# Three layers on one core: the order of the second layer's operands, one pair of weights split from PSUM, and two weight tiles converted ahead

## The chip, the cores and the metric

The kernel runs on one core of a Trainium2 chip. The metric is the time of the device in microseconds (us), the median of several executions. The engines are called as in the profile: PE (TensorE, matrix products; PEld its weight loads), DVE (VectorE), ACT (ScalarE), POOL (GpSimd) and SP (SyncE, which issues the transfers). Each engine works through its own list of instructions in order and waits where an instruction needs another engine's result.

## The reference

```python
def reference(q, k, v, p, w_in, w_out, w_gate, w_val, w_out2):      # shortened
    # q, k, v: (4, 8, 576, 64); p: (4, 8, 32, 64)
    pp = sm_attn(p, k, v)                       # softmax attention, 32 packed rows
    a = sm_attn(q, pp, pp)                      # (4, 8, 576, 64)
    x = a.transpose(0, 2, 1, 3).reshape(2304, 512)
    h = x @ w_in                                # 512 x 2048
    x = softplus(h) @ w_out                     # 2048 x 512
    return (sigmoid(x @ w_gate) * (x @ w_val)) @ w_out2   # 512 x 1536, 1536 x 512
```

The inputs of the attention are float32, the five weights are float64.

## The kernel before

**Precision.** A product is made of three matmuls on fp32r operands: each operand x is split in hi, a copy rounded to fp32r, and lo = x - hi, and `mm3` adds hi·hi, hi·lo and lo·hi. `split_lo` (line 99) is the subtraction, on VectorE or GpSimd. The weights come in as float64 bits; `convert` makes float32 of a block with three integer operations on VectorE (lines 178, 183, 187), 128x512 each.

**First layer.** The batch b and the half s of its tokens select 288 tokens; `emit_h(b, c, s)` makes 256 of the 2048 columns of h (chunk c, eight chunks) and `emit_out1` adds their share of the output to `xa` (six matmuls, then the addition of line 658 on VectorE, four PSUM banks in turn). The second attention product and w_in are joined: instead of x, the kernel takes the attention weights (A2h, A2l) and multiplies them by pp @ w_in, which `prep_wp_one` (one batch) or `prep_wp_two` (two batches, a "half") makes for each chunk: four small matmuls for either of two banks (line 587), then hi and lo of the result (wph, wpl). In `prep_wp_two` ScalarE copies PSUM to SBUF (cv, line 594), GpSimd makes hi (line 102) and GpSimd makes lo (line 99). From chunk 2 on the batches go in two halves (batches 0, 1 and batches 2, 3), chunk by chunk.

**Second layer.** For each pair of f (128 columns of w_gate and of w_val; twelve f) and each half ps of the batches, x @ w_gate and x @ w_val are made together from seven products of half size and additions (Strassen's scheme as Winograd orders it). With x of a batch as four quarters x11, x12 (first half of the tokens) and x21, x22 (second half), the operands of the tokens' side ("A operands", tiles aop) are A11 = x11, A12 = x12, A22 = x22, S1 = x21 + x22, S2 = S1 - x11, S4 = x12 - S2 and S3 = x11 - x21; `prep_A(b)` makes the four sums on VectorE (line 705), all hi on ScalarE (line 698) and all lo on VectorE, that of A22 on GpSimd. The weights' side (BH, BL) comes from `blocks(f)`, which converts three raw tiles (raw_g, raw_v, raw_o), builds four further blocks with GpSimd subtractions and stores the result to a scratch in DRAM for the second half, and from `prep_B(ps, f)`, which reloads the scratch if there is one and splits it (GpSimd: hi of some, all lo; w_out2's are oh and ol). `emit_gv` multiplies in the order A11, S2, S3, S1, A12, A22, S4; each product needs one of three double banks, which VectorE's additions (lines 927, 939) and ScalarE's copies set free. `emit_out2` multiplies the gated result gv by w_out2's block, twice 128 columns at a time, and adds it to `xa` (line 982).

**What sets the order.** The work of preparation is written as generators in the queues `jobs` and `idle`; `tick()`, called after each piece of TensorE's work, takes one step of the first job, so a job that stands ahead delays those behind it. Blocks for the f in the list `EARLY` are converted ahead, in layer 1, from chunk 4 on. The tile framework's scheduler then puts the instructions of each engine in its own order, so the order in the program isn't that of the source. At the passage from ps = 0 to ps = 1, f = 11 is done batch by batch, and `prep_A` of batches 2 and 3 is put in the queue behind batch 0 and 1.

Of the kernel before, what the change touches and what calls it, by code (L numbers as in the profile page):

```python
# [9 lines left out]
F32 = mybir.dt.float32  # L10
# [3 lines left out]
ALU = mybir.AluOpType  # L14
# [6 lines left out]
def attn_moe_moe_kernel(  # L21
# [21 lines left out]
    nc = tc.nc  # L43
# [5 lines left out]
    P = 128  # L49
    NC = 6  # L50
    CT = S // NC
    HS = S // 2
# [14 lines left out]
    XR = 0  # L67
    VCH = 8
    VSP = 0
    EARLY = [0]  # L70
    NCV = 5
    SC = float(D) ** -0.5

# [55 lines left out]
    later = {f: [(nm, f // 2, f % 2) for nm in ("g", "v", "o2")] for f in range(2 * NCH2)}  # L129
    early = list(EARLY)  # L130
    order, early_in = [], {}
# [114 lines left out]
    jobs = deque()  # L246
# [42 lines left out]
    WPP = 1  # L289
    WPH = 0  # L290
    SPL = []
    SP0 = []
    ALO = ['A22']
    EV2 = EM2 = EM1 = [nc.vector, nc.vector]
    EGL = [nc.gpsimd, nc.vector]
    HIA = [5, 9]
# [242 lines left out]
    def x2(b, s):  # L539

        i = KD * HS * (2 * b + s)
        return xa[:, i : i + KD * HS].rearrange("p (m t) -> p m t", m=KD)
# [35 lines left out]
    def prep_wp_two(half, c):  # L578
        wt = w_in_f[c]
        hl = [wp_tiles() for _ in range(2)]  # L580
        if WPP:
            xs = [new_cv().rearrange("p (t n) -> p t n", t=2) for _ in range(2)]
        for par in range(2):
            ps = bank1().rearrange("p (t n) -> p t n", t=2)
            for t in range(2):
                j = 2 * t + par
                nc.tensor.matmul(  # L587
                    ps[:, t, :], bdT[:, 4 * half + j, :], wt[:, j, :], start=True, stop=True
                )
            yield  # L590
            for e in range(2):
                r = slice(64 * e, 64 * e + 64)
                if WPP:
                    nc.scalar.activation(xs[e ^ par][r], ps[r], AF.Copy)
                else:
                    hi, lo = hl[e ^ par]
                    nc.scalar.activation(hi[r], ps[r], AF.Copy)
                    split_lo(nc.vector, lo[r], ps[r], hi[r])
                yield
            yield  # L600
        if WPP:
            for (hi, lo), x in zip(hl, xs):
                hi_of(WPH, hi, x)
                split_lo(nc.gpsimd, lo, x, hi)
                yield
        for x in range(2):
            Wp[2 * half + x, c] = hl[x]
# [69 lines left out]
    w2 = []  # L677
    NF = NCH2 * 2
    HB = B // 2
    Aop, Bop, scratch, gv = {}, {}, {}, {}  # L680

    def prep_A(b):
        pool = w2[0] if b % 2 == 0 else big
        n = 11 if pool is big else 7
        Aop[b] = {}
        for nms in (("A11", "A12"), ("A22", "S1"), ("S2", "S3"), ("S4",)):
            tiles = [
                pool.tile([P, 2, 2, HS], F32R, tag="big", bufs=n, name="aop")
                for _ in range(len(nms))
            ]  # L690
            for e, nm in enumerate(nms):
                Aop[b][nm] = [tiles[0][:, e], tiles[-1][:, 1 if len(nms) == 1 else e]]
        x11, x12 = x2(b, 0)[:, :2], x2(b, 0)[:, 2:]
        x21, x22 = x2(b, 1)[:, :2], x2(b, 1)[:, 2:]

        def split(nm, x):
            hi, lo = Aop[b][nm]
            nc.scalar.activation(hi, x, AF.Copy)
            split_lo(nc.gpsimd if nm in ALO else nc.vector, lo, x, hi)

        def sum_():
            return w2[0].tile([P, 2, HS], F32, tag="sum", name="sum")

        def tt(to, x, y, op):
            nc.vector.tensor_tensor(to, x, y, op=op)

        split("A11", x11)
        yield
        split("A12", x12)
        yield  # L710
        split("A22", x22)
        yield
        t = sum_()
        tt(t, x21, x22, ALU.add)
        yield
        split("S1", t)
        yield
        tt(t, t, x11, ALU.subtract)
        yield
        split("S2", t)  # L720
        yield
        tt(t, x12, t, ALU.subtract)
        yield
        split("S4", t)
        yield
        t = sum_()
        tt(t, x11, x21, ALU.subtract)
        yield
        split("S3", t)
        yield  # L730


# [49 lines left out]
    def prep_B(ps, f):  # L782

        if f in scratch:
            parts = [new_cv(), new_cv()[:, :CF], new_cv(), new_cv(), new_cv()]
            for x, a, n in places(parts):
                nc.sync.dma_start(x, scratch[f][:, a : a + n])
        else:
            parts = yield from blocks(f)
        yield  # L790
        pool = w2[f % 2]
        hi = pool.tile([P, 7 * CF], F32R, tag="BH", name="BH")
        lo = pool.tile([P, 7 * CF], F32R, tag="BL", name="BL")
        oh = wo_p.tile([P, DM], F32R, tag="woh", bufs=4, name="oh")
        ol = wo_p.tile([P, DM], F32R, tag="wol", bufs=4, name="ol")
        for x, a, n in places(parts):
            h, l = (oh, ol) if a == 7 * CF else (y[:, a : a + n] for y in (hi, lo))
            hi_of(HIA[ps] * 100 > a, h, x)
            split_lo(nc.gpsimd, l, x, h)
            yield  # L800
        Bop[ps, f] = (
            hi.rearrange("p (j n) -> p j n", n=CF), lo.rearrange("p (j n) -> p j n", n=CF),
            oh, ol,
        )
# [27 lines left out]
    for i, (b, c) in enumerate(entries):  # L832
        if c == 0:
            while not att_done(2 * b + 1):
                att_tick()
            if b:
                for cc in range(2):
                    jobs.appendleft((f"wp{b}{1 - cc}", prep_wp_one(b, 1 - cc)))
        if (b, c) == (3, 0):
            jobs.append(("win2", prep_win(2)))  # L840
        if (b, c) == (3, 1):
            jobs.append(("wp02", prep_wp_two(0, 2)))
        if c >= 2 and b % 2 == 0:
            k = groups.index((b // 2, c))
            if k == 0:
                jobs.append(("wo2", prep_wo(2)))
            if k + 1 < len(groups):
                x, cc = groups[k + 1]
                jobs.append((f"wp{2 * x}{cc}", prep_wp_two(x, cc)))
            if k + 2 < len(groups) and weights and groups[k + 2][1] == weights[0]:  # L850
                cc = weights.popleft()
                jobs.extend(idle)
                idle.clear()
                jobs.append((f"win{cc}", prep_win(cc)))
                jobs.append((f"wo{cc}", prep_wo(cc)))
                idle.append((f"early{cc}", prep_early(early_in.get(cc, ()))))
            if (b, c) == BAT:
                jobs.extend(idle)
                idle.clear()
                jobs.append(("B00", prep_B(0, 0)))  # L860
        for x in range(2):
            if (b, c) == (x + 2, NCH1 - 2):
                jobs.append((f"A{x}", prep_A(x)))
        if (b, c) == CPC:
            cps[0] = CPS > 0
        if (b, c) == (1, 2):
            att.release()
            w2.append(tc.alloc_tile_pool(name="w2", bufs=1, side="right"))
        finish(f"wp{b}{c}" if c < 2 else f"wp{b - b % 2}{c}")
        for s in range(2):  # L870
            emit_h(b, c, s)
            pace = 0
            for bb in range(b + 1, B if c < 2 else 0):
                slots = 3 * (4 * bb - 2 * i - s) - MARGIN
                pace = max(pace, -(-att_left(2 * bb + 1) // max(1, slots)))
            ticks = [pace] * 3
            if len(pend) == DEPTH:
                emit_out1(*pend.popleft(), ticks)
            else:
                for m in range(KD):  # L880
                    between(m, ticks)
            pend.append((b, c, s))
# [119 lines left out]
    for i, (ps, f) in enumerate(steps):  # L1002
        finish(f"B{ps}{f}")
        if i + 1 < len(steps):
            n_ps, n_f = steps[i + 1]
            jobs.append((f"B{n_ps}{n_f}", prep_B(n_ps, n_f)))
        whole = list(range(HB))
        first_last = f in (SPL if ps else (SP0 + [NF - 1]))
        for n, group in enumerate([[p] for p in whole] if first_last else [whole]):
            for p in group:  # L1010
                finish(f"A{HB * ps + p}")
            emit_gv(ps, f, group)
            if ps == 0 and f == NF - 1:
                jobs.appendleft((f"A{HB + n}", prep_A(HB + n)))
            some_out2(LEFT if n or not first_last else LEFT0)
        if f % 2:
            todo.extend((ps, f // 2, t) for t in range(NTT))
            spread[0] = -DEL
# [37 lines left out]
```

## Time and profile before

| what | value |
|---|---|
| time, median of 3 runs (lowest to highest) | 868.61 us (866.66 to 870.32) |
| profiled execution: time / span | 866.77 / 864.7 us |
| TensorE (PE) busy, granted clock | 839.6 us (97%), 1.000 |
| weight loads (PEld) busy | 789.6 us (91%) |
| VectorE (DVE) busy | 614.6 us (71%) |
| ScalarE (ACT) busy | 401.1 us (46%) |
| GpSimd (POOL) busy | 473.2 us (55%) |

The span is the time from the first to the last instruction that the trace holds. Busy times of different engines overlap. An engine that is busy for a part of the span can still be the one that is waited for in some stretch; that is read from the waits of that stretch. The first layer's last addition lies at 435.9 us, the passage from ps = 0 to ps = 1 between 616 and 655 us.

### The profile page before, as it was taken

Reading aid. Unit: us, or ns where it says so; the run is one execution under the profiler, and the core shown is the slowest. Engines: PE = TensorE matmul, PEld = TensorE weight load, DVE = VectorE, ACT = ScalarE, POOL = GpSimd, SP = SyncE. Lnnn points to the kernel's source line nnn. Section 1 sums busy time; section 2 is a strip of 40 time slices with the busy share of each in tenths; the row PEclk is TensorE's granted clock in tenths of the full one; section 3 lists DMA queues with packets and bytes.
Section 4 is the critical chain, followed back from the end, with each engine's and each line's share of the span. In section 5 each row is a group of like instructions: output and inputs, shape, how many; then the busy total and the mean of one; then the engine's idle time right before and its main releaser. Section 6 shows DMA issues by size and latency. Waiting matters only on the chain.

```text
span 864.7 us, 15615 instructions
## 1 busy us (share of the span) xinstructions
PE 839.6 (97%) x6100; PEld 789.6 (91%) x6100; DVE 614.6 (71%) x1047; ACT 401.1 (46%) x721; POOL 473.2 (55%) x455
## 2 busy tenths in 40 slices
PE   6899999999999999999999999999989999999997
PEld 5788999989999999999999999999869999999995
DVE  1875556757576767758898688897898756767665
ACT  4567565566666666677633422232342532322210
POOL 4454233346565545576479787796883634536400
PEclk9999999999999999999999999999999999999999
DMA  9983330113032402300057464554434212213004
GB/s 233 229 221 84 80 83 2 50 49 99 1 98 92 135 21 79 123 30 1 1 167 215 134 192 148 170 136 157 140 95 137 79 45 86 67 43 111 14 1 109
DMA packets 58009, 85.55 MB, mean 99 GB/s; under 512 B 6352, under 2 KB 39248, under 8 KB 57936
## 3 DMA queue, kind: packets, MB, share of 16 engines
q1 hardware_dynamic: 57648, 84.49, 34.5%
q8 instruction: 48, 0.79, 0.4%
q14 instruction: 25, 0.20, 0.1%
q10 hardware_dynamic: 288, 0.07, 0.0%
HBM read 65.67 MB, written 18.87 MB: 98 GB/s over the span
## 4 chain that ended last, share of the span: by engine, by line
PE 84%; DVE 7%; DMA 3%; ACT 2%; POOL 2%; issue 1%; SPq 0%; POOLq 0%; ACTq 0%; DVEq 0%
PE bank L113 9%; PE bank L111 9%; PE bank L112 9%; PE ps L650 7%; PE ps L651 7%; PE ps L653 7%; PE ps L976 5%; PE ps L975 5%; PE ps L974 5%; PE ps L113 4%; PE ps L111 4%; PE ps L112 4%; PE ps L587 2%; DVE aop L99 2%; PE ps L464 2%; PE ps L348 1%
## 5 line engine op out<-in xcount | busy, mean ns | idle before, releaser
L111 PE MATMUL bank<-aop,BH 128*128 128x288 f32 x672 | 198.7, 296 | 2.8 <-DVE work L927 1.1
L112 PE MATMUL bank<-aop,BH 128*128 128x288 f32 x672 | 197.9, 295 | 1.0 <-DVE aop L99 0.9
L113 PE MATMUL bank<-aop,BL 128*128 128x288 f32 x672 | 198.7, 296 | 0.1
L99 POOL TENSOR_TENSOR ghl<-g,ghl 128x576 fp32r<-128x576 f32 x64 | 93.7, 1464 | 131.5 <-ACT ghl L106 131.5
L658 DVE TENSOR_TENSOR xa<-xa,ps 128x288 f32<-128x288 f32 x224 | 98.1, 449 | 75.4 <-PE ps L653 75.3
L650 PE MATMUL ps<-ghl,woh 128*128 128x288 f32 x512 | 148.6, 305 | 1.6 <-DVE xa L658 1.5
L651 PE MATMUL ps<-ghl,wol 128*128 128x288 f32 x512 | 143.2, 295 | 0.0
L111 PEld LDWEIGHTS bank<-aop,BH 128*128 128x128 f32 x672 | 126.2, 188 | 8.0 <-issue 1.2
L112 PEld LDWEIGHTS bank<-aop,BH 128*128 128x128 f32 x672 | 126.4, 188 | 5.1 <-DVE aop L99 1.6
L113 PEld LDWEIGHTS bank<-aop,BL 128*128 128x128 f32 x672 | 126.5, 188 | 0.4 <-POOL BL L99 0.4
L99 POOL TENSOR_TENSOR BL<-cv,BH 128x512 fp32r<-128x512 f32 (+1 forms) x96 | 117.7, 1242 | 7.2 <-ACT BH L106 6.1
L653 PE MATMUL ps<-ghl,woh 128*128 128x288 f32 x512 | 109.1, 294 | 0.0
L650 PEld LDWEIGHTS ps<-ghl,woh 128*128 128x128 f32 x512 | 96.2, 188 | 4.1 <-DVE xa L658 1.3
L651 PEld LDWEIGHTS ps<-ghl,wol 128*128 128x128 f32 x512 | 96.3, 188 | 0.6
L927 DVE TENSOR_TENSOR work<-work,bank 128x576 f32<-128x576 f32 (+1 forms) x100 | 70.9, 724 | 28.6 <-PE bank L113 28.1
L974 PE MATMUL ps<-oh,gv 128*128 128x512 f32 x216 | 84.6, 392 | 1.3 <-DVE xa L982 0.8
L975 PE MATMUL ps<-ol,gv 128*128 128x512 f32 x216 | 84.8, 393 | 0.0
L976 PE MATMUL ps<-oh,gv 128*128 128x512 f32 x216 | 84.7, 393 | 0.0
L653 PEld LDWEIGHTS ps<-ghl,woh 128*128 128x128 f32 x512 | 82.2, 188 | 0.0
L982 DVE TENSOR_TENSOR xa<-xa,ps 128x512 f32<-128x512 f32 x90 | 61.5, 684 | 27.1 <-PE ps L976 26.6
L956 ACT ACTIVATE work<-bank 128x576 f32<-128x576 f32 (+1 forms) x25 | 15.8, 634 | 137.4 <-DVE bank L927 137.4
L113 PE MATMUL ps<-A2h,wpl 128*128 128x288 f32 x256 | 76.2, 297 | 2.4 <-POOL wpl L99 2.0
(123 smaller groups left out, 1743.6 us busy)
## 6 DMA issues: line engine op xcount, KB each, us to landing
cv<-B SPq DMA_DIRECT2D x52, 256.0 KB, 2.6
B<-cv SPq DMA_DIRECT2D x48, 256.0 KB, 3.8
raw_in<-in_moe_w_in_dram SPq DMA_DIRECT2D x16, 512.0 KB, 3.6
raw_out<-in_moe_w_out_dram SPq DMA_DIRECT2D x16, 512.0 KB, 3.6
raw_g<-in_moe_w_gate_dram SPq DMA_DIRECT2D x12, 512.0 KB, 4.2
raw_v<-in_moe_w_val_dram SPq DMA_DIRECT2D x12, 512.0 KB, 4.4
raw_o<-in_moe_w_out_dram SPq DMA_DIRECT2D x12, 512.0 KB, 4.1
xa<-in_q_dram SPq DMA_DIRECT2D x6, 576.0 KB, 6.5
```

The costliest lines, as they stand in the source:

```text
L99: eng.tensor_tensor(lo, x, hi.bitcast(F32), op=ALU.subtract)
L111: nc.tensor.matmul(ps, wh, xh, start=first, stop=False)
L112: nc.tensor.matmul(ps, wh, xl, start=False, stop=False)
L113: nc.tensor.matmul(ps, wl, xh, start=False, stop=last)
L650: nc.tensor.matmul(out_, wh[:, ms], gh[:, f], start=f == 0, stop=False)
L651: nc.tensor.matmul(out_, wl[:, ms], gh[:, f], start=False, stop=False)
L653: nc.tensor.matmul(out_, wo_hl[c, f][0][:, ms], gl[:, f], start=False, stop=f == 1)
L658: nc.vector.tensor_tensor(dst, dst, out_, op=ALU.add)
L927: nc.vector.tensor_tensor(to, x, y, op=ALU.add)
L974: nc.tensor.matmul(bank, gh[:, ts_], oh, start=f == 0, stop=False)
L975: nc.tensor.matmul(bank, gh[:, ts_], ol, start=False, stop=False)
L976: nc.tensor.matmul(bank, gl[:, ts_], oh, start=False, stop=f == 1)
```

## The change

`EARLY` becomes `[0, 1]`, so the blocks of f = 0 and of f = 1 are converted in layer 1 (f = 1 in the chunks that follow those of f = 0), stored to the scratch and reloaded by `prep_B(0, 1)`. `prep_wp_two` takes the splits straight from PSUM for half 0, chunk 2 only: ScalarE writes hi and VectorE subtracts it from PSUM. In `prep_A` the operands are made in the order in which `emit_gv` multiplies by them. S2 is made in place of x21 by a new job `fold_A` (two operations); S3 = x22 - S2 and S1 = S2 + x11 follow from it. That is five sums and folds for each batch instead of four. The jobs F0 and F1 stand right ahead of A0 and A1; F2 and F3, for batches 2 and 3, are queued at f = 3 and f = 5 of ps = 0.

```diff
-    EARLY = [0]
+    EARLY = [0, 1]
...
+    FOLD = {3: 2, 5: 3}
...
     def prep_wp_two(half, c):
...
-        if WPP:
+
+        far = WPP and (half, c) != (0, 2)
+        if far:
             xs = [new_cv().rearrange("p (t n) -> p t n", t=2) for _ in range(2)]
...
-                if WPP:
+                if far:
                     nc.scalar.activation(xs[e ^ par][r], ps[r], AF.Copy)
                 else:
                     hi, lo = hl[e ^ par]
...
-        if WPP:
+        if far:
             for (hi, lo), x in zip(hl, xs):
...
+    def fold_A(b):
+
+        x11, x12, x21, x22 = quarters(b)
+        tt(x21, x21, x22, ALU.add)
+        yield
+        tt(x21, x21, x11, ALU.subtract)
+        yield
+
     def prep_A(b):
...
-        for nms in (("A11", "A12"), ("A22", "S1"), ("S2", "S3"), ("S4",)):
+        for nms in (("A11", "S2"), ("S3", "S1"), ("A12", "A22"), ("S4",)):
...
         split("A11", x11)
         yield
+        split("S2", s2)
+        yield
+        t = sum_(x22, s2, ALU.subtract)
+        yield
+        split("S3", t)
+        yield
+        t = sum_(s2, x11, ALU.add)
+        yield
+        split("S1", t)
+        yield
         split("A12", x12)
         yield
         split("A22", x22)
         yield
-        t = sum_()
-        tt(t, x21, x22, ALU.add)
...
+        t = sum_(x12, s2, ALU.subtract)
         yield
         split("S4", t)
-        yield
-        t = sum_()
-        tt(t, x11, x21, ALU.subtract)
-        yield
-        split("S3", t)
         yield
...
+                jobs.append((f"F{x}", fold_A(x)))
                 jobs.append((f"A{x}", prep_A(x)))
...
+        if ps == 0 and f in FOLD:
+            jobs.append((f"F{FOLD[f]}", fold_A(FOLD[f])))
```

In the whole program VectorE has 8 rows of instructions more (987 to 995), SyncE 7 more, ScalarE and GpSimd one each, TensorE as many as before. What the scheduler makes of it is shown at three places; the number ahead of a row is its place in the engine's list. The line numbers of the new program are higher by 3 to 14: its 590, 653 to 656, 661 are the old 587, 650 to 653, 658, its 690 the old 705, its 941, 953 and 996 the old 927, 939 and 982.

First, TensorE at the weights of chunk 6, half 0. A row with w_in is the second product pp @ w_in, ghl with woh is out1, A2h with wph is an H block. Before:

```order
1596 L587 MATMUL ps_4304<-w_in,bdT 128x256 x2
1597 L650 MATMUL ps_4307<-ghl,woh 128x288
1598 L651 MATMUL ps_4307<-ghl,wol 128x288
...
1602 L111 MATMUL ps_4316<-A2h_100,wph 128x288
1603 L112 MATMUL ps_4316<-A2l_104,wph 128x288
...
1646 L650 MATMUL ps_4392<-ghl,woh 128x288
...
1661 L111 MATMUL ps_4442<-A2h_97,wph 128x288
1662 L112 MATMUL ps_4442<-A2l_101,wph 128x288
1663 L113 MATMUL ps_4442<-A2h_97,wpl 128x288
```

And in the new program:

```order
1644 L590 MATMUL ps_4398<-w_in,bdT 128x256 x2
1645 L653 MATMUL ps_4418<-ghl,woh 128x288
1646 L654 MATMUL ps_4418<-ghl,wol 128x288
...
1660 L653 MATMUL ps_4449<-ghl,woh 128x288
1661 L654 MATMUL ps_4449<-ghl,wol 128x288
1662 L653 MATMUL ps_4449<-ghl,woh 128x288
...
1665 L111 MATMUL ps_4465<-A2h_97,wph 128x288
1666 L112 MATMUL ps_4465<-A2l_101,wph 128x288
1667 L113 MATMUL ps_4465<-A2h_97,wpl 128x288
```

Before, two H blocks of another batch (A2h_100) and eight out1 tiles stand between the product with w_in and the first H block with the new weights (A2h_97), 72 matmuls; now four out1 tiles do, 24 matmuls.

Second, VectorE at the end of layer 1, among the additions of the last out1 tiles (xa<-xa,ps). Before:

```order
577 L632 SCALAR_TENSOR_TENSOR g_5449<-ps_5405,t_5418 128x576
578 L705 TENSOR_TENSOR sum<-xa 128x576
579 L658 TENSOR_TENSOR xa<-xa,ps_5456 128x288
580 L658 TENSOR_TENSOR xa<-xa,ps_5466 128x288
581 L99 TENSOR_TENSOR aop<-sum,aop 128x576
582 L658 TENSOR_TENSOR xa<-xa,ps_5474 128x288
...
586 L178 TENSOR_SCALAR ps_5556<-raw_g 128x512
587 L658 TENSOR_TENSOR xa<-xa,ps_5506 128x288
588 L183 SCALAR_TENSOR_TENSOR ps_5556<-raw_g,ps_5556 128x512
589 L658 TENSOR_TENSOR xa<-xa,ps_5514 128x288
590 L658 TENSOR_TENSOR xa<-xa,ps_5522 128x288
```

In the new program:

```order
589 L635 SCALAR_TENSOR_TENSOR g_5481<-ps_5436,t_5449 128x576
590 L661 TENSOR_TENSOR xa<-xa,ps_5488 128x288
591 L661 TENSOR_TENSOR xa<-xa,ps_5498 128x288
592 L690 TENSOR_TENSOR sum<-xa 128x576
593 L99 TENSOR_TENSOR aop<-xa,aop 128x576
594 L661 TENSOR_TENSOR xa<-xa,ps_5508 128x288
595 L99 TENSOR_TENSOR aop<-sum,aop 128x576
596 L661 TENSOR_TENSOR xa<-xa,ps_5518 128x288
...
600 L661 TENSOR_TENSOR xa<-xa,ps_5550 128x288
601 L178 TENSOR_SCALAR ps_5730<-raw_g 128x512
602 L661 TENSOR_TENSOR xa<-xa,ps_5558 128x288
603 L183 SCALAR_TENSOR_TENSOR ps_5730<-raw_g,ps_5730 128x512
```

Before, one A operand's split and a sum stand behind the last `g` (the softplus, line 632 or 635), and then the conversion of f = 1's raw_g; now two splits and a sum follow a sum, and the conversion is that of f = 2 and comes with the last addition.

Third, VectorE at the passage from ps = 0 to ps = 1, from the first A operand of batch 2 on (work and bank are the additions behind products, xa<-xa,ps of 128x512 is the second layer's output). Before:

```order
806 L99 TENSOR_TENSOR aop<-xa,aop 128x576
807 L927 TENSOR_TENSOR work<-work,bank 128x288 x2
808 L99 TENSOR_TENSOR aop<-xa,aop 128x576
809 L982 TENSOR_TENSOR xa<-xa,ps_7704 128x512
810 L927 TENSOR_TENSOR bank<-work,bank 128x288
811 L99 TENSOR_TENSOR aop<-sum,aop 128x576
812 L982 TENSOR_TENSOR xa<-xa,ps_7722 128x512
813 L927 TENSOR_TENSOR bank<-work,bank 128x288
814 L705 TENSOR_TENSOR sum<-sum,xa 128x576
815 L982 TENSOR_TENSOR xa<-xa,ps_7740 128x512
816 L939 TENSOR_TENSOR work<-work,bank 128x288
```

In the new program:

```order
811 L99 TENSOR_TENSOR aop<-xa,aop 128x576 x2
812 L996 TENSOR_TENSOR xa<-xa,ps_7689 128x512
813 L941 TENSOR_TENSOR work<-work,bank 128x288 x3
814 L99 TENSOR_TENSOR aop<-sum,aop 128x576
815 L996 TENSOR_TENSOR xa<-xa,ps_7720 128x512
816 L941 TENSOR_TENSOR bank<-work,bank 128x288
817 L690 TENSOR_TENSOR sum<-xa 128x576
818 L996 TENSOR_TENSOR xa<-xa,ps_7738 128x512
819 L99 TENSOR_TENSOR aop<-sum,aop 128x576
820 L941 TENSOR_TENSOR bank<-work,bank 128x288
821 L99 TENSOR_TENSOR aop<-xa,aop 128x576
```

The operands of batch 2 stood in the order A11, A12, S1, with S2's sum behind; now A11 and S2 come at once, then S3, S1 and A12.

## Rows read from the trace of the kernel before

**Rows 1.** TensorE's waits: engine, line, releaser: us in total, times, longest.

```profile
PE ps L113 <- POOL wpl L99: 2.0, 1, 2.0
...
PE ps L650 <- DVE xa L658: 1.5, 3, 0.6
...
PE bank L111 <- DVE xa L658: 0.7, 1, 0.7
...
PE bank L111 <- POOL ol L99: 0.5, 1, 0.5
```

**Rows 2.** Stretches: TensorE, weight load, VectorE, ScalarE, GpSimd busy; clock; DMA share; GB/s.

```profile
620.00:660.00 40.00, 36.60 (x208) 31.36 (x207) 37.12 (x53) 13.79 (x27) 24.55 (x19) 1.00 0.40 116
660.00:680.00 20.00, 20.00 (x153) 20.00 (x152) 16.75 (x20) 8.44 (x16) 14.25 (x12) 1.00 0.32 92
```

**Rows 3.** Timeline of TensorE, chunks 2 and 6 of half 0: start, us, instruction [idle before].

```profile
173.27 1.02 PE L587 MATMUL ps<-w_in,bdT 128*128 128x256 f32 x4
173.94 0.49 PE L650 MATMUL ps<-ghl,woh 128*128 128x288 f32 x1
...
177.52 0.29 PE L653 MATMUL ps<-ghl,woh 128*128 128x288 f32 x1
179.81 0.40 PE L113 MATMUL ps<-A2h,wpl 128*128 128x288 f32 x1 [2.00 <-POOL wpl L99]
...
333.96 1.02 PE L587 MATMUL ps<-w_in,bdT 128*128 128x256 f32 x4
```

**Rows 4.** Timeline of ScalarE, chunk 2 of half 0.

```profile
174.67 1.19 ACT L594 ACTIVATE cv<-ps 64x512 f32<-64x512 f32 x2
```

**Rows 5.** Timeline of GpSimd, chunks 2 and 6 of half 0.

```profile
175.94 1.21 POOL L102 TENSOR_SCALAR wph<-cv 128x512 fp32r<-128x512 f32 x2 [2.97 <-PE ps L653]
177.12 1.42 POOL L99 TENSOR_TENSOR ghl<-g,ghl 128x576 fp32r<-128x576 f32 x1
178.49 2.51 POOL L99 TENSOR_TENSOR wpl<-cv,wph 128x512 fp32r<-128x512 f32 x2
...
337.76 1.21 POOL L102 TENSOR_SCALAR wph<-cv 128x512 fp32r<-128x512 f32 x2
```

**Rows 6.** Groups by line and shape, VectorE, whole span.

```profile
L99 DVE TENSOR_TENSOR wpl<-ps,wph 128x512 fp32r<-128x512 f32 x8 | 5.5, 682 | 4.4 <-ACT wph L573 4.4
```

**Rows 7.** Timeline of VectorE, end of layer 1.

```profile
419.90 1.74 DVE L705 TENSOR_TENSOR sum<-sum,xa 128x576 f32<-128x576 f32 x1
...
424.35 1.52 DVE L99 TENSOR_TENSOR aop<-sum,aop 128x576 fp32r<-128x576 f32 x1 [0.60 <-ACT aop L698]
...
427.48 0.76 DVE L99 TENSOR_TENSOR aop<-sum,aop 128x576 fp32r<-128x576 f32 x1
...
430.69 1.42 DVE L99 TENSOR_TENSOR aop<-sum,aop 128x576 fp32r<-128x576 f32 x1
...
433.49 0.68 DVE L178 TENSOR_SCALAR ps<-raw_g 128x512 int32<-128x512 int32 x1
```

**Rows 8.** Timeline of GpSimd, end of layer 1.

```profile
419.20 1.82 POOL L99 TENSOR_TENSOR ol<-cv,oh 128x512 fp32r<-128x512 f32 x1
...
437.25 1.62 POOL L99 TENSOR_TENSOR BL<-cv,BH 128x512 fp32r<-128x512 f32 x1 [5.75 <-ACT BH L106]
```

**Rows 9.** VectorE's lo splits (line 99), 616 to 655 us: busy (count).

```profile
616.00:655.00 39.00, 14.04 (x12) 1.00 0.40 115
```

**Rows 10.** VectorE's sums (line 705), 616 to 655 us: busy (count).

```profile
616.00:655.00 39.00, 7.18 (x7) 1.00 0.40 115
```

**Rows 11.** Groups by line and shape, VectorE, 616 to 655 us.

```profile
L982 DVE TENSOR_TENSOR xa<-xa,ps 128x512 f32<-128x512 f32 x15 | 10.2, 680 | 2.4 <-PE ps L976 2.3
...
L927 DVE TENSOR_TENSOR work<-work,bank 128x288 f32<-128x288 f32 x8 | 3.4, 444 | 0.3 <-PE bank L113 0.2
```

**Rows 12.** Timeline of TensorE, second layer's output.

```profile
646.97 0.39 PE L975 MATMUL ps<-ol,gv 128*128 128x512 f32 x1
647.20 0.39 PE L976 MATMUL ps<-oh,gv 128*128 128x512 f32 x1
```

More of the change, by code (lines that the diff above doesn't have):

```diff
@@ L680, in attn_moe_moe_kernel, with quarters, tt @@
     Aop, Bop, scratch, gv = {}, {}, {}, {}
+    def quarters(b):
+        x1, x2_ = x2(b, 0), x2(b, 1)
+        return x1[:, :2], x1[:, 2:], x2_[:, :2], x2_[:, 2:]
+    def tt(to, x, y, op):
+        nc.vector.tensor_tensor(to, x, y, op=op)
+    def fold_A(b):
[4 more added lines that the diff above has]
+        yield
     def prep_A(b):
@@ L692, in prep_A @@
                 Aop[b][nm] = [tiles[0][:, e], tiles[-1][:, 1 if len(nms) == 1 else e]]
-        x11, x12 = x2(b, 0)[:, :2], x2(b, 0)[:, 2:]
-        x21, x22 = x2(b, 1)[:, :2], x2(b, 1)[:, 2:]
+        x11, x12, s2, x22 = quarters(b)
         def split(nm, x):
@@ L699, in split, with sum_ @@
             split_lo(nc.gpsimd if nm in ALO else nc.vector, lo, x, hi)
[L701 to L705, printed above, removed]
+        def sum_(x, y, op):
+            t = w2[0].tile([P, 2, HS], F32, tag="sum", name="sum")
+            tt(t, x, y, op)
+            return t
         split("A11", x11)
+        yield
[8 more added lines that the diff above has]
+        split("S1", t)
         yield
@@ L712, in prep_A @@
         yield
-        t = sum_()
-        tt(t, x21, x22, ALU.add)
-        yield
-        split("S1", t)
-        yield
[L718 to L722, printed above, removed]
+        t = sum_(x12, s2, ALU.subtract)
         yield
         split("S4", t)
-        yield
-        t = sum_()
-        tt(t, x11, x21, ALU.subtract)
-        yield
-        split("S3", t)
         yield
```

## The prediction

> **What bounds the kernel.** The profiled execution took 866.77 us for a span of 864.7, 1.84 us below the median of the runs shown (868.61); terms are summed against 866.77 and the 1.84 is put back at the end. TensorE is busy for 97% of the span at a granted clock of 1.000 (its full 2.4 GHz level), and the change leaves its number of instructions as it is. So only the time in which TensorE stands still can move. I read the list of its waits first, then the table of stretches, then the timelines around each wait. The reader is to see four places [rows 1, 2]: 2.0 us at one matmul that waits for GpSimd's wpl; 1.5 + 0.7 us at the end of the first layer, where VectorE's adds into xa are late; 0.5 us soon after, for GpSimd's ol; and 40.00 - 36.60 = 3.4 us where the second layer passes from batches 0 and 1 to batches 2 and 3. That is 8.1 us, 0.94% of the time, and all that this change can win: in the rest of the two layers TensorE is busy throughout. A wait costs about 0.1 us more than its row says, as the matmul behind it also lasts 0.40 instead of 0.29 us [rows 3].
>
> **First edit: one pair's weights straight from PSUM, for batches 0 and 1, chunk 2.** Before, the second product pp @ w_in ends at 173.27 + 1.02 = 174.29 and the third product of the H block, the first that reads wpl, starts at 179.81. The one before it started at 177.52, so at 0.131 us a matmul (153 in 20 us where TensorE is never idle [rows 2]) 179.81 - 177.52 - 0.13 = 2.16 us are lost [rows 3]. In between stand ScalarE's two copies to SBUF, to 175.86 [rows 4], and on GpSimd two hi (1.21 us), a ghl subtraction (1.42) and the wpl subtractions (2.51 for two) [rows 5]. The edit takes GpSimd out: ScalarE's two 64-row copies write hi at the same 1.19 us, and VectorE makes the lo from PSUM. A 64x512 split is not in the trace; its bounds are zero and the 0.68 us of the 128x512 one [rows 6], and I take the upper one, since ScalarE's 64-row copies at 0.6 us are no shorter per column. In the new program the last lo follows one short copy on VectorE, and eleven matmuls (1.45 us) lie on TensorE between the out1 tile that this copy waits for and the product that wants the lo; 0.17 + 0.40 + 0.68 = 1.25 us is in time. I leave 0.1 us of wait. **Term 1: -2.05 us** (-2.16 to -1.5, where 0.68 us is late once).
>
> **What that moves.** The other pairs keep the far way, and the conversions of f = 1 now stand in the queue of jobs ahead of chunk 6's weights. By the order of TensorE's program its second product with w_in lies only 24 matmuls ahead of the H block of (0,6), where before 72 stood. From the end of that product the far way needs 1.57 us for the copies (to 175.86), 0.08, then 1.21 for two hi, 1.26 for the first wpl and 0.07, thus 4.19 us if no ghl stands between [rows 4, 5], and none does in the new order. TensorE comes to the same place after 3.1 to 3.5 us: 26 matmuls by 0.13, less the 0.35 by which it goes on before the product's end (173.94), and up to 0.43 more for the gaps that (0,2) showed. The rest, 0.7 to 1.1 us, is new waiting. Before, in this very pair, hi began 2.8 us after the product's end (334.98 to 337.76) and not 1.65, as a ghl was ahead of it [rows 3, 5]; one is ahead in the new order too, and if it is as late, 1.1 us more are lost. I stay near the price without it. **Term 2: +1.0 us** (0 if ScalarE and GpSimd come early; 2.2 with that ghl in the way).
>
> **The end of the first layer.** TensorE makes an out1 tile of six matmuls in 0.78 us; VectorE adds it in some 0.4 and does everything else in the rest, so each extra instruction there is TensorE's loss. Before, between the last fourteen adds stand five operations on A operands, 1.52, three of 0.75 to 0.76 (the row at 427.48 stands for them) and 1.42 us, together 5.21, and two conversion steps at 0.68 [rows 7]; the two at 1.4 to 1.5 lie beside a GpSimd subtraction, the other three do not. In the new order there are six such operations and one conversion step. At the same prices, with 1.5, 0.76, 0.76 and 0.75 for the first four and 1.4 for the last two, which have GpSimd's f = 1 operands and a ghl beside them, that is 6.57 + 0.68 = 7.25 against 6.57 us. **Term 3: +0.7 us.** The lower end is six quiet ones, 6 x 0.75 + 0.68 - 6.57 = -1.4; the upper one has the last three at 1.95 us, the price of GpSimd's own A subtraction, about +3.0. GpSimd stood idle from 431.5 to 437.25 here [rows 8]; in the new order it works through it.
>
> Why company costs: the sum at 419.90 took 1.74 us instead of 0.75 beside the GpSimd subtraction of 419.20 to 421.02 [rows 7, 8]. The Trainium skill (SBUF — State Buffer, section "SBUF: two separate sides") says that VectorE instructions with two SBUF inputs and GpSimd share one port pair as an exclusive lock: whoever starts first holds it for its whole instruction and the other blocks. By that rule the sum would end at 421.02 + 0.75 = 421.77, and the trace has 421.64, so it agrees here. It speaks against moving GpSimd's work next to VectorE's splits; with every late split blocked, term 3 would be its upper end rather than +0.7.
>
> **Conversions ahead.** The 9 conversion steps of f = 1 (0.68 us each), 4 GpSimd subtractions and 5 stores move to chunks 5 and 6, where TensorE has no wait in the list; five reloads on SyncE's queue come in, issued with those of f = 0, well before they are wanted. They cost nothing while VectorE has its slack there; term 2 is what they cost through the queue of jobs. What they give is the wait for ol, 0.48 us and the 0.1 behind it. **Term 4: -0.55 us** (-0.6 to 0). VectorE has five instructions fewer in the first two steps of f, with four in-place folds added; TensorE does not wait for VectorE there, so I put it at nothing (with no slack each fold would cost 0.75 us).
>
> **From batches 0, 1 to 2, 3.** Before, matmuls of the second layer's output, held back, filled TensorE while VectorE made 12 lo splits and 7 sums. The new order of operands lets the scheduler put 78 matmuls of products in a row, with only three of the output's ahead of them. Of VectorE's work up to the last split (S4 of batch 3) 12 splits, 5 sums, 18 half-width adds, 4 full ones and 5 out2 adds stand from the second product of batch 0 at f = 11 on. At the means of this stretch, 14.04/12 = 1.17 us for a split [rows 9] and 7.18/7 = 1.03 for a sum [rows 10], with 0.42 for a half add (0.44 less its overlap) and 0.66 for an out2 add [rows 11], and 0.75 for a full one, as any quiet operation of that size, that is 14.0 + 5.2 + 7.6 + 3.0 + 3.3 = 33.1 us. TensorE in the same piece has 150 matmuls of 288 columns by 0.131 and 36 of 512 by 0.228 [rows 12], 27.9 us, from 0.3 us earlier. So it must wait for 33.1 - 27.6 = 5.5 us, less if the last four operations find GpSimd quiet as it was there before (4 x 0.35 = 1.4). I take 4.3 us against 3.4 + five times 0.1 = 3.9 lost before, rounded to **term 5: +0.3 us**. Quiet throughout, 17 operations at 0.75, VectorE needs 26.7 us, less than TensorE's 27.6, and nothing is lost: -3.9 us. With the full 5.5 it is +1.6.
>
> **Sum:** -2.05 + 1.0 + 0.7 - 0.55 + 0.3 = -0.6 us; 866.77 - 0.6 + 1.84 = 868.0 us.
>
> **Rivals.** A, *both passages come free*: operands in the order of the products mean that TensorE gets S2 and S3 as it wants them, and VectorE mostly finds GpSimd out of the way. Terms 1 and 4 stand, term 2 is 1.0, term 3 -1.4, term 5 -3.9: -6.9 us, 861.7 us. For it: a quiet split is at 0.76 [rows 7], and 17 quiet operations fit. Against it: GpSimd's list of work there is nearly the same as before, and the same splits took 1.17 on the mean.
>
> B, *slower*: VectorE's splits wait out GpSimd's instructions between the halves, with no output matmuls left to fill TensorE. Some 12 of the 17 operations stand where GpSimd was at work before; at 1.83 us (an aop subtraction's wait plus its own 0.75, near the 1.74 and 1.52 seen at the end of layer 1 [rows 7]) rather than 1.1 that is 12 x 0.73 = +8.8 us, 876.8 us. It turns the sign by more than 0.5% when these 12 last above 1.1 + 4.9/12 = 1.51 us on the mean. The lock quoted above is this rival's rule; the mean of 1.17 for this stretch's splits [rows 9] holds it to a lesser price so far.
>
> C, *the wait only moves*: chunk 6 gets the whole wait that chunk 2 had, with a late ghl ahead of hi. Term 2 is 2.2 and the sum +0.6, 869.2 us, so that the first edit has bought nothing. For it: the same 25 matmuls or so of margin, and the late hi that this pair had before [rows 5]. Against: no ghl stands between hi and lo in the new order, as one did at 177.12.
>
> **Chances.** My forecast with its near neighbours (864.5 to 870.5) 0.47, A 0.26, C 0.17, B 0.10. This kernel's measurement tells about 0.5% from no change, so faster means below 864.3 and slower above 872.9: A and a little of the forecast make 0.28, B 0.10, the rest 0.62. The range takes in A and the upper bounds of terms 2, 3 and 5 in part: 861.0 to 871.5.
>
> **What will show it.** Term 1: the wait for wpl at about 180 us is gone, and 64x512 splits from PSUM show near 0.68 us. Term 2: a wait of a product for GpSimd's wpl of 0.7 to 2 us in chunk 6, at some 345 us. Term 3: waits for xa of 2 to 3 us in the last ten us of layer 1, with late splits at 1.4. Term 4: no wait for ol at 449. Term 5: TensorE idle by 3 to 4.5 us between 620 and 660, in waits for aop and work, with splits at 1.1 to 1.2. I am wrong if those splits are all at 0.75 (then A) or past 1.5 (then B), or if the moved conversions make TensorE wait in chunks 5 and 6, where I put nothing.

## The result, and the profile after

The changed kernel takes 873.42 us in the median of 7 runs (872.28 to 877.33), the kernel before 868.48 beside it (866.07 to 870.32): 1.0067 times as long, 95% interval 1.0054 to 1.0081. It is slower by 0.7%, and 873.42 lies outside the range of the prediction. The profiled execution took 874.87 us for a span of 873.1. TensorE's waits, by line and releaser (us in total, times, longest):

```profile
PE ps L653 <- DVE xa L661: 6.1, 7, 1.5
...
PE ps L990 <- POOL gv L99: 1.1, 1, 1.1
PE ps L113 <- POOL wpl L99: 1.0, 1, 1.0
...
PE bank L111 <- DVE xa L661: 0.7, 1, 0.7
PE ps L656 <- POOL ghl L99: 0.7, 1, 0.7
PE bank L111 <- ACT work L958: 0.6, 1, 0.6
PE ps L988 <- DVE xa L996: 0.6, 1, 0.6
```

Of the entries that the change was to remove [rows 1], wpl is down from 2.0 to 1.0 us (at another place) and ol is gone. But VectorE's adds into xa (line 661, the old 658), at 1.5 us before, now hold TensorE for 6.1 us, in seven waits. Where that is shows in a table of stretches; the first product of the second layer starts at 435.91 us before and at 444.59 after, and bounds the third row and the fourth. Columns as in [rows 2]; the stretch less TensorE's busy time is its idle time. Before:

```profile
140.00:200.00 60.00, 57.53 (x468) 55.14 (x467) 37.16 (x76) 36.00 (x60) 24.87 (x21) 1.00 0.11 36
200.00:385.00 185.00, 185.00 (x1355) 182.87 (x1355) 126.30 (x248) 122.45 (x193) 105.58 (x94) 1.00 0.25 79
385.00:435.91 50.91, 48.72 (x359) 47.61 (x357) 44.12 (x75) 32.24 (x51) 26.29 (x18) 1.00 0.00 1
435.91:500.00 64.09, 63.48 (x435) 60.76 (x436) 52.45 (x79) 25.53 (x41) 55.81 (x62) 1.00 0.63 185
600.00:680.00 80.00, 76.60 (x487) 70.01 (x486) 69.30 (x96) 30.20 (x55) 57.85 (x51) 1.00 0.41 122
```

After:

```profile
140.00:200.00 60.00, 59.37 (x481) 56.94 (x480) 42.34 (x82) 36.37 (x61) 21.95 (x19) 1.00 0.12 36
200.00:385.00 185.00, 181.93 (x1322) 178.59 (x1321) 128.11 (x252) 119.82 (x189) 106.17 (x95) 1.00 0.31 94
385.00:444.59 59.59, 53.96 (x388) 51.71 (x386) 51.93 (x80) 35.28 (x56) 34.70 (x26) 1.00 0.07 21
444.59:500.00 55.41, 53.78 (x368) 51.09 (x369) 45.25 (x64) 19.57 (x31) 44.14 (x47) 1.00 0.50 150
600.00:680.00 80.00, 78.20 (x492) 71.64 (x491) 65.98 (x98) 29.03 (x53) 54.08 (x47) 1.00 0.38 113
```

| stretch | idle before | idle after | change |
|---|---|---|---|
| 140 to 200 us | 2.47 | 0.63 | -1.84 |
| 200 to 385 us | 0 | 3.07 | +3.07 |
| 385 us to the first product | 2.19 | 5.63 | +3.44 |
| first product to 500 us | 0.61 | 1.63 | +1.02 |
| 600 to 680 us (passage) | 3.40 | 1.80 | -1.60 |

These five add up to +4.1 us, and some 0.1 us behind each of six more waits (19 instead of 13 from 130 us on) brings it near the +4.9 of the medians. The attention up to 62 us differs by 1.4 us more between these two profiles (11.0 and 12.4 us idle), but it ran from 10.0 to 12.5 in the profiles of this study, whatever the kernel, so that is not the change's.

TensorE's five waits between 200 and 430 us, in its timeline:

```profile
332.61 0.37 PE L653 MATMUL ps<-ghl,woh 128*128 128x288 f32 x1 [0.59 <-DVE xa L661]
...
347.49 0.40 PE L113 MATMUL ps<-A2h,wpl 128*128 128x288 f32 x1 [0.99 <-POOL wpl L99]
...
360.79 0.37 PE L653 MATMUL ps<-ghl,woh 128*128 128x288 f32 x1 [1.36 <-DVE xa L661]
...
402.52 0.40 PE L653 MATMUL ps<-ghl,woh 128*128 128x288 f32 x1 [1.49 <-DVE xa L661]
...
411.05 0.37 PE L653 MATMUL ps<-ghl,woh 128*128 128x288 f32 x1 [1.12 <-DVE xa L661]
```

### The profile page after: what moved, and what is told of

Read it like the earlier page. It is cut to its first block, busy times and chain, and to the rows that moved or that the text cites. A ratio compares the mean times of both kernels' runs of the same rounds, so it can differ in the third digit from the quotient of the medians.

```text
span 873.1 us, 15644 instructions
## 1 busy us (share of the span) xinstructions
PE 842.1 (96%) x6100; PEld 789.8 (90%) x6100; DVE 625.7 (72%) x1055; ACT 400.3 (46%) x721; POOL 473.9 (54%) x451
## 5 line engine op out<-in xcount | busy, mean ns | idle before, releaser
L111 PE MATMUL ps<-A2h,wph 128*128 128x288 f32 x256 | 78.1, 305 | 0.2
```

The lines of the kernel that those rows point to most:

```text
L111: nc.tensor.matmul(ps, wh, xh, start=first, stop=False)
```

## The experiments

A ratio is to runs of the kernel before on the same chip. "Idle" is TensorE's, by the stretches of the table.

**The parts alone and one part undone.** The first runs were to tell whether the parts' costs stand where the profile shows them.

`e1_no_early`, the changed kernel with

```diff
-    EARLY = [0, 1]
+    EARLY = [0]
```

> The changed kernel with EARLY back at [0]; the new operand order with its folds and the split from PSUM stay. Theory (each part costs where it stands): the stall of chunks 5 and 6 (about +4.2 us between the 160th and the 200th addition to xa) goes, the one at the end of layer 1 (about +5 us) stays, the passage between the halves keeps its gain of 2; against before -1.7 + 5 - 2 = +1.3 us, 869 to 871 us. Rival (the moved conversions push the A operands late, so that the stalls at 400 to 411 us are theirs too): all of the loss goes, -1.7 - 2 = -3.7 us, about 865 us.

Measured: 872.21 us, 1.0041 (1.0024 to 1.0059). The idle time from 200 to 385 us went from 3.07 to 0.12, and that to the first product stayed (5.61): the two losses are separate, as the theory says. The time fell less than it said (869 to 871 us): 2.46 us (not 1.63) were idle in the first steps of layer 2, and TensorE's granted clock fell just before and behind the first product:

```profile
420.00:430.00 10.00, 9.55 (x72) 9.34 (x71) 9.34 (x13) 6.15 (x10) 4.03 (x3) 1.00 0.01 2
430.00:440.00 10.00, 7.44 (x42) 6.34 (x41) 9.21 (x16) 2.41 (x4) 3.77 (x2) 0.84 0.00 0
440.00:450.00 10.00, 10.00 (x64) 10.00 (x65) 8.28 (x13) 2.94 (x4) 5.58 (x7) 0.81 0.51 147
450.00:460.00 10.00, 9.39 (x71) 9.19 (x70) 9.56 (x16) 3.61 (x6) 9.88 (x10) 1.00 0.67 202
```

The columns are those of the table of stretches; the last but two is the granted clock. With four short waits, 2.56 us of idle time in ten, it was 0.84 and then 0.81 on the mean, between the chip's two levels of 2.4 and 1.2 GHz.

`e2_direct_only`, the kernel before with `far = WPP and (half, c) != (0, 2)` alone.

> The kernel before with the split from PSUM for half 0, chunk 2 alone. Both theories: the wait for GpSimd's wpl near 180 us goes and nothing else moves, -1.7 to -2.1 us, 866.4 to 866.8 us. If the time stays at 868.5 the wait was hidden by something else.

Measured: 865.54 us, 0.9968 (0.9958 to 0.9978). Idle from 140 to 200 us 0.61, everything else as before. This part alone beats both kernels. The time is lower than expected: 2.8 us under the kernel before (1.9 to 3.6 by the interval), for 1.9 us of idle time that went.

`e3_early_only`, the kernel before with `EARLY = [0, 1]` alone.

> The kernel before with EARLY = [0, 1] alone. Theory: +4.2 us in chunks 5 and 6 (VectorE held by raw tiles that land late, and a product that waits for GpSimd's wpl), the wait for ol at 449 us gone, -0.5: about 872 us. Rival: the stalls at the end of layer 1 come with it, +8 us, about 876 us.

Measured: 876.31 us, 1.0090 (1.0069 to 1.0111), at the rival's time, but not for the rival's reason: the idle time to the first product is 2.46 us, as before (2.19). From 200 to 385 us it is 2.61, and 3.30 came in one wait in the first steps of layer 2. VectorE stood for a raw tile, with the additions behind two products queued after it:

```profile
454.62 0.70 DVE L178 TENSOR_SCALAR ps<-raw_v 128x512 int32<-128x512 int32 x1 [2.75 <-DMA raw_v<-in_moe_w_val_dram]
455.22 0.75 DVE L927 TENSOR_TENSOR bank<-work,bank 128x576 f32<-128x576 f32 x1
```

TensorE waited for those additions:

```profile
456.78 0.58 PE L111 MATMUL bank<-aop,BH 128*128 128x288 f32 x1 [3.30 <-DVE work L939]
```

After this gap the granted clock was 0.79 and 0.87 for two times ten us. That raw_v was late because its load stood behind three stores on SyncE is what the queue shows, but no run took it away.

`e4_order_only`, the changed kernel with `EARLY = [0]` and `far = WPP`, so the new operands and folds alone.

> The kernel before with the new operand order and its folds alone. Theory: +5 us at the end of layer 1, up to +0.9 in the first steps of layer 2, -2 at the passage between the halves: +3 to +4 us, 871.5 to 872.5 us. Rival: nothing at the end of layer 1 without the moved conversions, -2 us, 866.5 us.

Measured: 873.88 us, 1.0069 (1.0054 to 1.0084). Idle to the first product 5.58, passage 1.65: the theory's places, and more than its sum (3 to 4 us), with the clock at 0.83 in the ten us from 440.

**What makes VectorE late in layer 1.** `e5_stores_scalar` issues the stores of `blocks` by `nc.scalar.dma_start` instead of `nc.sync.dma_start`.

> The changed kernel with the stores of the converted blocks issued from ScalarE's queue instead of SyncE's. Theory (in chunks 5 and 6 VectorE is held by raw tiles whose loads were queued on SyncE behind these stores): the waits of VectorE for raw_in (1.3 us at 331) and raw_out (1.7 at 359) shrink and with them TensorE's 0.6 and 1.4 us; 2 us less than the changed kernel, about 871.5 us. Rival (the loads are late because a raw buffer comes free late, whatever the queue): the two waits stay, 873 to 874 us.

Measured: 874.79 us, 1.0077 (1.0062 to 1.0092). VectorE's two waits are 0.9 and 1.1 us instead of 1.3 and 1.7; the rival is nearer. The changed kernel's own trace says the same: the load of raw_out that VectorE waits for at 358.86 us was issued at 353.4, when the conversion of 352.69 us (0.68) had emptied a buffer, with no store ahead of it, and landed 5.4 us later. ScalarE's stores made a wait of their own, 3.02 us at 468 us.

`e12_early_last` puts the raw tiles of f = 1 behind those of chunk 7:

```diff
-            n = -(-len(early) // (NCH1 - c))
-            early_in[c], early = early[:n], early[n:]
+            early_in[c] = {4: [0], 7: [1]}.get(c, [])
```

> The changed kernel with the raw tiles of f = 1 put behind those of chunk 7 in the order of loads and conversions, instead of between chunks 5 and 6. Theory (two raw buffers serve all weights; f = 1's three tiles in between make chunk 6's and 7's raw tiles late, VectorE waits for them in order and its additions with it, and chunk 6's weights are made late): the waits for raw_in and raw_out and the one for wpl go, idle time from 200 to 385 us falls from 3.1 to under 0.5 us, 870.5 us. Rival (nine conversions more cost the same wherever they stand): as much is lost between 360 us and the first product, 873 us or more.

Measured: 870.76 us, 1.0043 (1.0024 to 1.0061):

```profile
200.00:385.00 185.00, 184.91 (x1355) 182.68 (x1354) 128.96 (x253) 121.81 (x192) 100.12 (x87) 1.00 0.26 80
385.00:438.13 53.13, 47.12 (x344) 45.67 (x342) 45.71 (x75) 32.97 (x52) 42.29 (x35) 1.00 0.24 73
438.13:500.00 61.87, 59.17 (x399) 55.90 (x400) 51.43 (x71) 22.34 (x36) 45.33 (x47) 1.00 0.44 135
```

Idle from 200 to 385 us is 0.09: neither VectorE nor the product waits there. The theory's place is right. Something comes back later, 6.01 and 2.70 against 5.63 and 1.63 us, about a half of what is won; why was not tried.

`e8_direct_last_pair`: `far = WPP and (half, c) not in ((0, 2), (1, 7))`.

> The changed kernel with the last pair's weights (half 1, chunk 7) split straight from PSUM too, so that GpSimd has no wph and wpl at 403 to 410 us while VectorE folds batch 1; VectorE gets four 0.68 us splits more. Theory (VectorE's sums, folds and splits there are long because they stand beside GpSimd's instructions): the two folds take 1.5 to 2.5 us instead of 3.74, TensorE's waits of 1.5 and 1.1 us at 402 and 411 go to under 1 us in all, 1.5 us less than the changed kernel, 872 us. Rival (VectorE simply has too many instructions there): four more make the waits longer, 874.5 us or more.

Measured: 873.74 us, 1.0076 (1.0047 to 1.0104): no change against the changed kernel. The two folds took 2.79 us instead of 3.74 and weren't quiet: a ghl subtraction took the place of wpl (a fold of 1.99 us at 414.17 beside a ghl of 413.65), and the 22 operations on the A operands took 27.7 us in all, as in the changed kernel. This run doesn't tell the theories apart, so the next one took more of GpSimd's work away.

`e9_quiet_gpsimd`: at the end of layer 1 ScalarE instead of GpSimd writes the lo of ghl (batches 2 and 3, chunks 6 and 7), of A22 (batches 0 and 1) and of the last pair's weights, as copies and not as differences, so their parts are left out of the result.

```diff
+            if b >= 2 and c >= 6:
+                nc.scalar.activation(gl, g32, AF.Copy)
+            else:
                 split_lo(nc.gpsimd if GLE else nc.vector, gl, g32, gh)
...
+            if nm in ALO and b < HB:
+                nc.scalar.activation(lo, x, AF.Copy)
+            else:
                 split_lo(nc.gpsimd if nm in ALO else nc.vector, lo, x, hi)
...
+                if (half, c) == (1, 7):
+                    nc.scalar.activation(hi, x, AF.Copy)
+                    nc.scalar.activation(lo, x, AF.Copy)
+                else:
```

> The changed kernel with GpSimd made quiet at the end of layer 1: the lo of ghl for batches 2 and 3 in chunks 6 and 7, the lo of A22 for batches 0 and 1 and hi and lo of the last pair's weights are left to ScalarE, which writes a rounded copy in place of each lo, so these lo parts are left out of the result. VectorE's instructions are the same. Theory (VectorE's sums, folds and splits are long there because GpSimd works beside them): they fall from 1.26 us on the mean to 0.75 to 0.9, TensorE's idle time from 385 us to the first product of layer 2 from 5.6 to 1.5 to 2.5 us, the time by 3 us to about 870.5. Rival (the number of VectorE's instructions sets it, or ScalarE's hi comes late): idle time stays above 4.5 us.

Measured: 866.08 us, 0.9977 (0.9966 to 0.9988), 7.3 us less than the changed kernel. VectorE's operations on the A operands, changed kernel (385 us to the first product; busy us, mean ns | idle before):

```profile
L99 DVE TENSOR_TENSOR aop<-xa,aop 128x576 fp32r<-128x576 f32 x6 | 9.2, 1554 | 0.6 <-ACT aop L716 0.6
...
L690 DVE TENSOR_TENSOR sum<-xa 128x576 f32<-128x576 f32 x6 | 6.4, 1059 | 0.1
L690 DVE TENSOR_TENSOR xa<-xa 128x576 f32<-128x576 f32 x4 | 6.3, 1580 | 0.1
L99 DVE TENSOR_TENSOR aop<-sum,aop 128x576 fp32r<-128x576 f32 x6 | 5.8, 975 | 0.8 <-ACT aop L716 0.6
```

The same 22 instructions with GpSimd quiet:

```profile
L99 DVE TENSOR_TENSOR aop<-xa,aop 128x576 fp32r<-128x576 f32 x6 | 5.3, 892 | 1.4 <-ACT aop L723 1.2
L99 DVE TENSOR_TENSOR aop<-sum,aop 128x576 fp32r<-128x576 f32 x6 | 5.2, 871 | 2.0 <-ACT aop L723 1.9
L697 DVE TENSOR_TENSOR sum<-xa 128x576 f32<-128x576 f32 x6 | 4.5, 754 | 0.1
L697 DVE TENSOR_TENSOR xa<-xa 128x576 f32<-128x576 f32 x4 | 4.1, 1034 | 0.1
```

They take 19.1 instead of 27.7 us, 0.87 instead of 1.26 us on the mean. And TensorE's idle time falls to 2.03 and 0.24 us:

```profile
385.00:438.30 53.30, 51.27 (x377) 50.02 (x375) 41.38 (x77) 41.20 (x68) 12.93 (x13) 1.00 0.07 18
438.30:500.00 61.70, 61.46 (x420) 58.77 (x421) 50.15 (x74) 23.55 (x38) 47.64 (x49) 1.00 0.46 138
```

The theory holds and the rival (the number of instructions) falls: with the number unchanged the stretch loses no more than before. The time fell by more than the theory's 3 us: 3.6 us of idle time went in this stretch and 1.4 in the next; the rest was not traced to a place.

**What the order and the folds do.** `e6_old_operands_01` makes the operands of batches 0 and 1 by the `prep_A` of before (EARLY = [0], split from PSUM kept):

```diff
-                jobs.append((f"F{x}", fold_A(x)))
-                jobs.append((f"A{x}", prep_A(x)))
+                jobs.append((f"A{x}", prep_A_old(x)))
```

> Direct split kept, EARLY = [0], and the operands of batches 0 and 1 made in the order of before; the new order with folds for batches 2 and 3 alone, where the folds stand in layer 2. Theory (the operand order costs at the end of layer 1 and gives at the passage between the halves): the stalls at 395 to 411 us and the extra ones before the first product go, the passage keeps its gain: -2.8 - 2 = -4.8 us against before, 863.5 us. Rival (the gain at the passage needs the folds and operands of all batches, or the folds in the first steps of layer 2 cost as much): 865.5 us or more.

Measured: 870.39 us, 1.0023 (1.0013 to 1.0032). Idle to the first product is 2.15, as before, so the new operands of batches 0 and 1 make that loss; but the first steps of layer 2 have 2.25 us (0.60 in e2) and the passage doesn't keep its gain, so the time is the rival's:

```profile
600.00:680.00 80.00, 76.10 (x475) 70.08 (x474) 67.20 (x95) 30.04 (x55) 54.30 (x49) 0.98 0.38 107
```

`e7_early_old_operands_01` adds `EARLY = [0, 1]` to it.

> The same with EARLY = [0, 1]. Theory (conversions ahead cost by themselves, about 4 us in chunks 5 and 6 and up to 4 more in the first steps of layer 2 where a raw tile is late): 5 to 8 us more than the run with EARLY = [0], 869 to 872 us. Rival (they cost only beside the direct split or before the old order of all batches): within 1.5 us of it.

Measured: 871.81 us, 1.0041 (1.0027 to 1.0056), 1.4 us more than e6, the rival's. The conversions ahead cost 2.11 us from 200 to 385 us and take 2.25 to 0.58 in the first steps of layer 2:

```profile
438.69:500.00 61.31, 60.73 (x413) 57.71 (x414) 49.92 (x71) 23.88 (x38) 45.94 (x50) 1.00 0.47 137
```

In that stretch, with the folds there, f = 1 is better converted ahead than not; in the whole it isn't.

`e10_reordered_no_folds` is e2 with the new pairing of tiles and four sums as before, in the order A11, S1, S2, S4, S3, A12, A22.

> The kernel before with the direct split, A12 and A22 made last and the tiles paired as in the changed kernel, but with the four sums of before and no folds (S1, S2, S4, S3). Theory (the fifth sum and the folds, that come in a burst, cost at the end of layer 1, not the order): TensorE's idle time from 385 us to the first product stays near 2.2 us, the passage between the halves lies between 1.8 and 3.4, 863.5 to 865.5 us. Rival (the order itself brings more of VectorE's work late): 867 us or more.

Measured: 869.65 us, 1.0009 (0.9999 to 1.0019). Idle to the first product is 2.31, as the theory says, but the time is the rival's: the passage has 4.98, and 3.23 of it stand at one out2 product behind VectorE.

`e11_pairing_only` is e2 with the new pairing alone.

> The kernel before with the direct split and only the tiles of the operands paired in the order of the products (A11 with S2, S3 with S1, A12 with A22), all operations as before. Theory (the gain at the passage comes from S2 and S3 being made early): nothing changes, 865.5 us. Rival (it comes from tiles that come free in the order in which they are wanted): TensorE's idle time at the passage falls from 3.4 to about 1.8 us, 863.9 us.

Measured: 867.96 us, 1.0000 (0.9983 to 1.0016). The passage has 3.75, so the rival (1.8) falls; but 3.25 us are idle to the first product, where one wait for xa grew from 0.58 to 1.64 us, which the theory did not have. The pairing alone gives nothing.

`e13_pairs_and_late_order` is e6 with the new pairing in `prep_A_old` too.

> The run with the old operand operations for batches 0 and 1 (direct split, EARLY = [0], new order with folds for batches 2 and 3), with the tiles of batches 0 and 1 paired as in the changed kernel too. Theory (the passage gains when S2 is folded ahead and its tile comes free in the order of the products, both together): TensorE's idle time from 600 to 680 us falls from 3.9 to about 1.8 us, 868.3 us. Rival (the passage gains from the operands of batches 0 and 1 being made in the new order): it stays at 3.4 to 4 us, 870.4 us.

Measured: 867.87 us, 0.9995 (0.9983 to 1.0007):

```profile
600.00:680.00 80.00, 78.27 (x498) 72.09 (x497) 67.84 (x98) 30.52 (x56) 58.56 (x51) 1.00 0.38 111
```

1.73 us: the passage has the changed kernel's gain again, with its order of TensorE's products (78 in a row). The pairing and the new operations of batches 2 and 3 (their folds ahead and their order, not told apart) make it together. The kernel as a whole gains nothing by it, since 3.22 us are idle to the first product, as with the pairing in e11, and 2.46 in the first steps of layer 2.

## Why the prediction was wrong

**Term 1, the split from PSUM (-2.05 us): right.** 1.84 us of idle time went, and alone it gave 0.9968. The splits took 0.67 to 0.69 us, by the upper bound:

```profile
172.47 0.67 DVE L99 TENSOR_TENSOR wpl<-ps,wph 64x512 fp32r<-64x512 f32 x1
...
178.94 0.69 DVE L99 TENSOR_TENSOR wpl<-ps,wph 64x512 fp32r<-64x512 f32 x1
```

**Term 2, chunk 6 (+1.0): right, with some luck in its parts.** The wait for wpl at 347.49 is 0.99 us. The copies were done 1.25 us after the product's end and not 1.57, and two ghl subtractions held the first hi from 344.35 to 344.99, which is rival C's condition in small; the two nearly cancel.

**Conversions ahead ("cost nothing while VectorE has its slack there"): the first step that failed.** Idle time from 200 to 385 us is 3.07, 2.1 of it not term 2's, at the place that the prediction itself had named as a sign of being wrong. VectorE had slack in time, but its instructions run in order and the ring of raw tiles has two buffers. With three tiles more in it, those of chunks 6 and 7 land late, and a conversion that waits for its load holds the additions behind it:

```profile
330.69 0.69 DVE L178 TENSOR_SCALAR ps<-raw_in 128x512 int32<-128x512 int32 x1 [1.29 <-DMA raw_in<-in_moe_w_in_dram]
...
332.02 0.45 DVE L661 TENSOR_TENSOR xa<-xa,ps 128x288 f32<-128x288 f32 x1
...
358.86 0.70 DVE L178 TENSOR_SCALAR ps<-raw_out 128x512 int32<-128x512 int32 x1 [1.72 <-DMA raw_out<-in_moe_w_out_dram]
...
360.19 0.45 DVE L661 TENSOR_TENSOR xa<-xa,ps 128x288 f32<-128x288 f32 x1
```

The numbers in brackets are VectorE's waits for the load; TensorE's at 332.61 and 360.79 end with the addition behind. With f = 1's tiles at the end of the ring, 0.09 us are left. The prediction had counted the moved instructions and SyncE's reloads, not what a late load does to the queue behind it.

**Term 3, the end of layer 1 (+0.7): the number met in its stretch, in part by luck, and the stretch was too short: the second step that failed.** Over the last fourteen additions, from 430 us on, the waits are 0.68 + 0.70 + 0.45 + 0.40 + 0.73 = 2.96 against 2.2 us before, +0.76. But VectorE's six operations and one conversion step there took 8.20 us, not 7.25, so 1.6 us more than before and not 0.7: not all of it was TensorE's loss, as the term had it, and the 0.70 is a wait for GpSimd's ghl. And 2.6 us more stand at 402.52 and 411.05, where the argument had not looked, as TensorE had no wait there before. VectorE there:

```profile
398.59 1.61 DVE L690 TENSOR_TENSOR sum<-xa 128x576 f32<-128x576 f32 x1
400.12 1.98 DVE L99 TENSOR_TENSOR aop<-xa,aop 128x576 fp32r<-128x576 f32 x1
402.03 0.44 DVE L661 TENSOR_TENSOR xa<-xa,ps 128x288 f32<-128x288 f32 x1
...
406.80 3.74 DVE L690 TENSOR_TENSOR xa<-xa 128x576 f32<-128x576 f32 x2
410.46 0.44 DVE L661 TENSOR_TENSOR xa<-xa,ps 128x288 f32<-128x288 f32 x1
```

and GpSimd:

```profile
398.17 1.42 POOL L99 TENSOR_TENSOR ghl<-g,ghl 128x576 fp32r<-128x576 f32 x1 [4.95 <-ACT ghl L106]
399.54 1.95 POOL L99 TENSOR_TENSOR aop<-xa,aop 128x576 fp32r<-128x576 f32 x1
...
406.23 1.95 POOL L99 TENSOR_TENSOR ghl<-g,ghl 128x576 fp32r<-128x576 f32 x1
408.13 1.79 POOL L99 TENSOR_TENSOR wpl<-cv,wph 128x512 fp32r<-128x512 f32 x1
```

Sum and split took 1.61 and 1.98 us, the two folds of batch 1 3.74, with no addition between them; each began beside a subtraction of GpSimd and ended 0.6 us behind one (the split at 402.10, the GpSimd one of 399.54 at 401.49). The fifth operation and the folds in a burst bring VectorE's work on the operands to 27.7 us (22 instructions; before it was 22.5 for 20 in the last sixty us of layer 1); with GpSimd quiet it is 19.1 and the loss is gone. This is rival B's mechanism, blocking beside GpSimd, at another place than B put it. The prediction should have weighed all the operations from 385 us on, not those of the last fourteen additions. By the rule of the exclusive lock in the Trainium skill (SBUF — State Buffer, section "SBUF: two separate sides") the second of two such instructions is blocked until the first is done. The ends agree with it here: a quiet operation of VectorE takes 0.75 us, and these ended 0.6 us behind GpSimd's.

**Term 4 (-0.55): wrong in sign.** The wait for ol went, but 1.02 us more are idle from the first product to 500 us: two waits for VectorE, 0.57 us together, and one of 1.06 us for GpSimd's gv. That "nothing" for the four folds held with f = 1 converted ahead: e7 has the folds and 0.58 us there. Without the conversions it doesn't (2.25 in e6, 0.60 in e2 without folds). The step that failed is that, for new waits, the term looked at VectorE alone: GpSimd worked from 455 to 481 us almost without a pause and made that gv late, and with part of its work at the end of layer 1 taken away the stretch has 0.24 (e9).

**Term 5, the passage (+0.3): wrong in sign.** -1.60 us. VectorE's 12 splits there took 1.07 us on the mean and not 1.17 (12.86 us in all), the 5 sums 0.93 and not 1.03, and the 44 operations of the tally ran from 626.78 to 656.15 us, in 29.4 us and not 33.1: it is the tally of VectorE's time that was too high. Of rival A's gain (-3.9) less than half came. It takes both the new operations of batches 2 and 3 and the pairing (e13); the pairing alone (e11) and another order without folds (e10) don't give it.

**The sum** has the idle times -1.84 + 3.07 + 3.44 + 1.02 - 1.60, +4.1 us, where the forecast had -2.05 + 1.0 + 0.7 - 0.55 + 0.3, -0.6.

## What to carry to other kernels

A step moved to a stretch "with slack" costs by what it puts ahead of others in an engine's queue and in a ring of buffers, not by its busy time; look for the next load of that ring and for who is queued behind the instruction that waits for it. An engine whose instructions last twice as long beside another's has no slack to be read off its busy share: take that other engine's work away once, and see what the stretch is worth. When a change has parts, time each alone: here the smallest edit (0.9968) was worth having, and the two others, each alone, cost more than it gave (1.0090 and 1.0069).

## What was not expected

TensorE's granted clock fell after waits that were each short. In the run without f = 1 converted ahead (e1) the longest wait between 425 and 440 us is 0.84 us, five waits add up to 3.0, and the clock was 0.84 from 430 to 440 us and 0.81 from 440 to 450; the changed kernel's profile, with 3.0 us idle from 430 to 450 us, stayed at 1.00. Its seven executions had mean clocks from 0.994 (877.33 us) to 1.000 (872.28 and 872.9), so a part of its median, and of its spread, is the clock's. What decides it was not tried.
